# Linear attention and a rational FFN on one core: weight bits joined by shift-and-or, attention from k and r in head pairs, remainders of the first slices on either of two engines, and the order of instructions written out as a list

## The chip, the cores and the metric

The kernel runs on one NeuronCore of a Trainium2 chip. The metric is the time of one execution on the device in microseconds; lower is better. Before the change three runs took 556.85, 558.38 and 558.58 us.

## The reference

Two stages. The first is a linear attention with a decaying state over 768 steps, for 4 batches of 8 heads with 48 dimensions; the second is a feed-forward layer with a rational function between two matrix products.

```python
for t in range(S):                       # B, H, S, D = 4, 8, 768, 48
    kt, vt, rt = (k[:, :, t], v[:, :, t], r[:, :, t])
    cur = np.einsum('bhd,bhe->bhde', u[None] * kt, vt)
    y[:, :, t] = np.einsum('bhd,bhde->bhe', rt, state + cur)
    state = w[None, :, :, None] * state + np.einsum('bhd,bhe->bhde', kt, vt)
...
h = x @ w_in                             # x: 3072 x 384, d_ff = 2048
h2 = h * h
h3 = h2 * h
P = a[0] + a[1] * h + a[2] * h2 + a[3] * h3
Q = 1.0 + np.abs(b[0]) * np.abs(h) + np.abs(b[1]) * h2
g = P / (Q + 1e-06)
return (g @ w_out).astype(np.float32)
```

Both weight matrices arrive as 64-bit floats, which the core sees as pairs of 32-bit words, so the kernel makes 32-bit floats of them out of their bits.

## The kernel before

**Attention.** The 3072 tokens are 24 blocks of 128 (block n is batch n % 4, piece n // 4); two blocks are a pair m, 12 pairs in all. For each block r, k and v are loaded, k and r are multiplied with tables of powers of w (`scale_k`, `scale_r`), the bonus term of u is formed (`bonus_a`, `bonus_b`, `bonus_sum`, `bonus_v`), and k and r are transposed in pairs of heads (`trans`): head q = 0 of a pair of heads comes to partitions 0 to 47, head q = 1 to partitions 64 to 111. `trr_ev` writes the transposed r into two tiles `ys[q]`, whose other partitions later take the masked products of k and r (`a_pe`, `a_ev`: four evictions of 64 partitions a pair). So one matmul over 128 partitions in `y_pe` sums the part of the state and the part of the block's own tokens: `vs` holds state rows and rows of v one above the other. `kv_pe` and `kv_ev` form the states (two chunks of 64 tokens, e = 0 and 1, apart for q), `carry` decays them, `y_ev` adds the bonus.

**Weights.** The two matrices are cut into 28 pieces (12 of 128 x 512 of w_in, 16 of 128 x 384 of w_out). For a piece `cv_load` brings the word pairs, `cv_exp` (ACT) rescales the upper word into PSUM (`cp`), `cv_shift` (DVE) shifts it by 3, `cv_up` and `cv_sign` (ACT) make a second tile `up` with the top bits of the lower word and the sign, and `cv_round` (POOL) adds the two as integers. For every fourth piece DVE puts the sign in (`cv_or`). `cv_hi` and `cv_lo` split the result into a high and a low half in a shorter format.

**FFN.** The tokens are 12 tiles of 256; a tile has 8 slices of 256 of the 2048 columns, 97 slices in all (the last one is cut in two). A slice is: the first product `f1` (tile 0 with whole 32-bit weights, `mm_full`; the others with three products of halves, `mm`), then on ACT Abs, two Squares, Ln and Exp (`ew_z`, `ew_q`, `ew_t`, `ew_ln`, `ew_exp`), on DVE four operations (`ew_u3`, `ew_hi`, `ew_p`, `ew_d`), the remainder `ew_lo` (DVE for slices 0 to 19, POOL from 20 on), and the second product `f2` (`mm2`), which sums up over a tile's slices into two PSUM banks.

**What sets the order.** Every step is a task with a list of what it depends on, of the buffers it takes (`new`) and gives back (`use`), and of the engines that may do it. Before, `order_of` played the program through with given durations and priorities (`PRM`: `OFF`, `CT`, `CS`, `AT`, `X`) and so chose each engine's order, the engine of each task and the PSUM bank; where PE had nothing to do between set times, it put in a matmul on constants (`warm`, line 1135). The engines then run their own lists strictly in order. PSUM has 5 banks `h`, one `pa` and two `o`.

Of the kernel before, what the change touches and what calls it, by code (L numbers as in the profile page):

```python
# [13 lines left out]
F32 = mybir.dt.float32  # L14
# [9 lines left out]
P = 128  # L24
# [5 lines left out]
SMALL = 2.0 ** -40  # L30

PRM = {'AT': (12.19, 36.51, 65.8, 109.86, 123.26, 133.52, 193.98, 232.99, 282.09, 313.75, 378.77, 401.82),
# [6 lines left out]
 'DUE': -79.79,  # L39
 'DX': 8.36,  # L40
 'FULL': (0,),
 'HFREE': 1,
 'MASKED': (),
 'MB': 149.17,
 'NSEG': 4,
 'NT': 1,
 'OFF': {'LV': 270.26,
         'Lk': 774.15,
         'Lr': -796.68,
         'Lv': -312.07,  # L50
         'a': -341.47,
         'ae': 398.71,
         'ba': 33.75,
         'bb': -348.95,
         'beta': -354.71,
         'bs': -201.32,
         'bv': -386.72,
         'c0': -322.33,
         'c2': 127.85,
         'c3': -103.81,  # L60
         'ca': -140.2,
         'ch': 121.32,
         'cl': -34.78,
         'cl_': -128.33,
         'co': -647.77,
         'coef': 293.84,
         'cr': 213.5,
         'cs': -175.01,
         'ctr': -337.17,
         'cu': -134.42,  # L70
         'd': -35.41,
         'ex': -222.41,
         'f1': -18.42,
         'f2': 29.16,
         'flag': -59.53,
         'flagm': 645.83,
         'flagt': 524.35,
         'hi': 12.18,
         'id': 91.47,
         'inv': -624.91,  # L80
         'kv': 150.51,
         'kve': -232.22,
         'ln': 63.38,
         'lo': -1043.9,
         'msk': 27.33,
         'od': 129.99,
         'os': -15.92,
         'p': 68.22,
         'pad': 25.39,
         'pl': 54.79,  # L90
         'pow': -277.52,
         'q': 362.68,
         'rest': 10.15,
         'sk': 150.8,
         'sq': -301.08,
         'sr': -807.06,
         'st0': 436.05,
         't': 292.34,
         'tab': -679.44,
         'tk': 221.19,  # L100
         'tke': 109.8,
         'tr': -205.98,
         'tre': 482.82,
         'turn': -129.33,
         'u3': -36.29,
         'ub': 38.7,
         'ube': -359.69,
         'ubp': -906.35,
         'uw': -294.57,
         'w': -428.73,  # L110
         'w128': -805.12,
         'wl': 257.36,
         'wp': 221.72,
         'x': -170.77,
         'xh': 511.5,
         'xl': 55.87,
         'y': -297.22,
         'ye': 218.13,
         'z': 276.11},
 'PORT': 0.02,  # L120
# [1137 lines left out]
```

## Time and profile before

| | us |
|---|---|
| median of 3 runs | 558.38 |
| lowest, highest | 556.85, 558.58 |
| the profiled execution | 556.55 |
| its span | 554.6 |
| PE busy | 528.4 (95%) |
| DVE busy | 465.9 (84%) |
| ACT busy | 427.8 (77%) |
| POOL busy | 262.9 (47%) |

The profile is of one execution. The span runs from its first instruction to its last; the execution's time is 1.95 us longer. Busy is the time in which an engine had at least one instruction running, and PE's includes the matmuls on constants (31.3 us). The mean granted clock of PE was 0.995 of full speed, and the core moved 35.53 MB. The windows cut the span into stretches with the busy time of each engine; a group's row gives line, engine, operation, output and inputs, count, then total busy us and mean ns of one, then the idle time just before.

### The profile page before, as it was taken

Reading aid. Unit: us, or ns where it says so; the run is one execution under the profiler, and the core shown is the slowest. Engines: PE = TensorE matmul, PEld = TensorE weight load, DVE = VectorE, ACT = ScalarE, POOL = GpSimd, SP = SyncE. Lnnn points to the kernel's source line nnn. Section 1 sums busy time; section 2 is a strip of 40 time slices with the busy share of each in tenths; the row PEclk is TensorE's granted clock in tenths of the full one; section 3 lists DMA queues with packets and bytes.
Section 4 is the critical chain, followed back from the end, with each engine's and each line's share of the span. In section 5 each row is a group of like instructions: output and inputs, shape, how many; then the busy total and the mean of one; then the engine's idle time right before and its main releaser. Section 6 shows DMA issues by size and latency. Waiting matters only on the chain.

```text
span 554.6 us, 14472 instructions
## 1 busy us (share of the span) xinstructions
PE 528.4 (95%) x5817; PEld 509.6 (92%) x5817; DVE 465.9 (84%) x736; ACT 427.8 (77%) x714; POOL 262.9 (47%) x255
## 2 busy tenths in 40 slices
PE   5999869899999999999999999999989999999996
PEld 4988658799999998999999999999989999999996
DVE  5999999899999889789788789688998696786773
ACT  7779888997785796685879585888665788888882
POOL 6766688857431164382445283334354232223221
PEclk9999999999999999999999999999999999999999
DMA  8664667235405007004005200007111000000001
GB/s 225 181 189 124 184 154 201 42 73 112 85 6 116 2 0 153 6 2 102 1 0 114 54 2 31 1 13 158 39 30 31 1 7 23 2 30 1 29 1 36
DMA packets 99503, 35.53 MB, mean 64 GB/s; under 512 B 92770, under 2 KB 95844, under 8 KB 99428
## 3 DMA queue, kind: packets, MB, share of 16 engines
q1 hardware_dynamic: 99428, 34.52, 25.8%
q8 instruction: 48, 0.79, 0.6%
q14 instruction: 27, 0.22, 0.1%
HBM read 29.79 MB, written 4.72 MB: 62 GB/s over the span
## 4 chain that ended last, share of the span: by engine, by line
PE 68%; DVE 20%; ACT 6%; issue 3%; POOL 1%; DMA 1%; SPq 0%; DVEq 0%; ACTq 0%; POOLq 0%
PE h L784 28%; PE o L794 10%; PE o L796 9%; PE o L795 9%; PE warm L1135 3%; DVE ys L703 3%; PE y L743 3%; DVE g L862 2%; DVE h L856 2%; DVE q L866 2%; DVE vs L732 2%; DVE h L872 1%; PE a L689 1%; PE x L760 1%; DVE ys L556 1%
## 5 line engine op out<-in xcount | busy, mean ns | idle before, releaser
L876 POOL TENSOR_TENSOR g<-q,z 128x512 fp32r<-128x512 f32 (+1 forms) x77 | 98.8, 1283 | 192.5 <-DVE q L872 147.0
L784 PE MATMUL h<-xth,whii 128*128 128x256 f32 x528 | 150.2, 284 | 0.0
L784 PE MATMUL h<-xth,wloi 128*128 128x256 f32 x528 | 147.5, 279 | 0.0
L784 PE MATMUL h<-xtl,whii 128*128 128x256 f32 x528 | 147.4, 279 | 0.0
L794 PE MATMUL o<-whio,g 128*128 128x384 f32 x384 | 134.7, 351 | 0.0
L795 PE MATMUL o<-wloo,g 128*128 128x384 f32 x384 | 130.1, 339 | 2.9 <-DVE wloo L553 2.9
L796 PE MATMUL o<-whio,g 128*128 128x384 f32 x384 | 130.2, 339 | 1.0 <-DVE g L876 1.0
L832 ACT ACTIVATE q<-h 128x512 f32<-128x512 f32 (+1 forms) x97 | 57.3, 591 | 77.0 <-PE h L784 76.7
L862 DVE SCALAR_TENSOR_TENSOR g<-h,sig,z 128x512 fp32r<-128x512 f32 (+1 forms) x97 | 72.0, 742 | 47.8 <-ACT z L852 46.2
L784 PEld LDWEIGHTS h<-xth,whii 128*128 128x128 f32 x528 | 99.3, 188 | 0.6
L784 PEld LDWEIGHTS h<-xtl,whii 128*128 128x128 f32 x528 | 99.3, 188 | 0.0
L784 PEld LDWEIGHTS h<-xth,wloi 128*128 128x128 f32 x528 | 99.2, 188 | 0.0
L856 DVE SCALAR_TENSOR_TENSOR h<-t,sig,h 128x512 f32<-128x512 f32 (+1 forms) x97 | 72.0, 743 | 7.4 <-ACT t L843 7.0
L866 DVE SCALAR_TENSOR_TENSOR q<-w,sig,g 128x512 f32<-128x512 f32 (+1 forms) x97 | 72.0, 742 | 5.5 <-DVE g L862 0.5
L795 PEld LDWEIGHTS o<-wloo,g 128*128 128x128 f32 x384 | 72.8, 190 | 3.5 <-DVE wloo L553 3.4
L838 ACT ACTIVATE w<-q,off,root 128x512 f32<-128x512 f32 (+1 forms) x97 | 75.6, 779 | 0.5 <-DVE g L876 0.5
L843 ACT ACTIVATE t<-h,off,root 128x512 f32<-128x512 f32 (+1 forms) x97 | 74.7, 771 | 0.2
L796 PEld LDWEIGHTS o<-whio,g 128*128 128x128 f32 x384 | 72.6, 189 | 1.9 <-DVE g L876 1.9
L794 PEld LDWEIGHTS o<-whio,g 128*128 128x128 f32 x384 | 72.6, 189 | 1.1 <-ACT whio L556 0.2
L848 ACT ACTIVATE z<-w,lnb 128x512 f32<-128x512 f32 (+1 forms) x97 | 66.4, 685 | 7.4 <-POOL m L648 0.4
L852 ACT ACTIVATE z<-z,lnb 128x512 f32<-128x512 f32 (+1 forms) x97 | 69.7, 719 | 2.4
L872 DVE SCALAR_TENSOR_TENSOR q<-h,sig,q 128x512 f32<-128x512 f32 (+1 forms) x77 | 57.0, 740 | 1.8
(147 smaller groups left out, 791.7 us busy)
## 6 DMA issues: line engine op xcount, KB each, us to landing
sti<-in_moe_w_in_dram SPq DMA_DIRECT2D x12, 512.0 KB, 4.8
sto<-in_moe_w_out_dram SPq DMA_DIRECT2D x16, 384.0 KB, 3.2
kh<-in_k_dram SPq DMA_DIRECT2D x24, 192.0 KB, 3.9
rh<-in_r_dram SPq DMA_DIRECT2D x24, 192.0 KB, 4.1
vn<-in_v_dram SPq DMA_DIRECT2D x24, 192.0 KB, 4.1
out_dram<-os SPq DMA_DIRECT2D x24, 192.0 KB, 2.0
vs<-in_v_dram SPq DMA_DIRECT2D x31, 96.0 KB, 3.3
wraw<-in_w_dram SPq DMA_DIRECT2D x1, 1.5 KB
```

The costliest lines, as they stand in the source:

```text
L784: nc.tensor.matmul(o, w_[nm][:, c], x_[:, cc], start=(n == 0), stop=(n == 3 * NCC - 1))
L794: nc.tensor.matmul(o, hi, w_["hi"], start=first, stop=False)
L795: nc.tensor.matmul(o, hi, w_["lo"], start=False, stop=False)
L796: nc.tensor.matmul(o, lo, w_["hi"], start=False, stop=last)
L838: nc.scalar.activation(g["w"], w_, AF.Square, scale=RB, bias=KB)
L843: nc.scalar.activation(g["t"], g["h"], AF.Square, scale=RA, bias=KA)
L848: nc.scalar.activation(g["z"], g["w"], AF.Ln, scale=2.0 ** -LN_SHIFT, bias=lnb[:, 2:3])
L852: nc.scalar.activation(g["z"], g["z"], AF.Exp, scale=-1.0, bias=lnb[:, 1:2])
L856: nc.vector.scalar_tensor_tensor(g["h"], g["t"], KAP, g["h"], op0=ALU.add, op1=ALU.mult)
L862: nc.vector.scalar_tensor_tensor(g["hi"], g["h"], c0, g["z"], op0=ALU.add, op1=ALU.mult)
L866: nc.vector.scalar_tensor_tensor(g["q"], g.get("w", g["q"]), qe, g["hi"].bitcast(F32), op0=ALU.add, op1=ALU.mult)
L876: e.tensor_mul(g["lo"], g["d"], g["z"])
```

## The change

Four things are changed.

1. Weights: `cv_round` on POOL is gone. `cv_join` on DVE shifts and ors in one instruction: `up` now holds bits that an or can set without a carry (scaled by 0.874 with 0.5 added). All 28 pieces take the sign from ACT; `cv_or` isn't used any more.
2. Attention: transposed r goes whole into one tile `rt`, as k does into `kt`; the masked products go to a tile `av` of 128 partitions (two evictions a pair), the states to `st` (one operation for both q), the odd heads' v with its halves of tokens swapped to `vo`, and the even heads' v is read where it was loaded. `y` is summed in two steps: `ys_pe` over the state (48 rows), `y_pe` over the block's own tokens (64 rows), into one PSUM bank for each q, where before there was one for each block. `a_ev` of q = 1 waits for `ys_pe`.
3. The remainder `ew_lo` of slices 0 to 19 may be on POOL or DVE and is written in place of q (`DYN`), as in the later slices.
4. `order_of` and its numbers are gone. `ORDER` is a list of 2194 task numbers, each with a letter for the engine where there is a choice; `placed` follows it. It has no entry for the matmul on constants.

```diff
-        nc.scalar.activation(dst, c["low"].bitcast(U32), AF.Copy, scale=2.0 ** -29)
+        nc.scalar.activation(dst, c["low"].bitcast(U32), AF.Copy, scale=UP * 2.0 ** -29, bias=0.5)
...
-    def cv_shift(c, p):
+    def cv_join(c, p):
         m = c["mag"].bitcast(I32)
         dst = m if on_vector(p) else cv_tile(c, "f", F32).bitcast(I32)
-        nc.vector.tensor_scalar(dst, m, 3, None, op0=ALU.logical_shift_left)
+        nc.vector.scalar_tensor_tensor(dst, m, 3, c["up"], op0=ALU.logical_shift_left, op1=ALU.bitwise_or)
...
-        return p % 4 == 0
+        return p in PRM["VEC"]
...
-    def cv_round(c):
-        bits = c["f"].bitcast(I32)
-        nc.gpsimd.tensor_tensor(bits, bits, c["up"], op=ALU.add)
...
-    def trr_ev(n, e, q):
-        copy(e, ys[q][RROWS[q], n % 2].rearrange("p a t -> p (a t)"), state[n]["tr"][RROWS[q]])
+    def trr_ev(n, e):
+        copy(e, rt[0:TR, n % 2].rearrange("p a t -> p (a t)"), state[n]["tr"][0:TR])
...
-                            ps[q][c, ts(x * NP + p, HALF)], kt[RROWS[q], x, p, c], ys[q][RROWS[q], x, p, c], start=True, stop=True
+                            ps[q][ts(e ^ q, HALF), ts(x * NP + p, HALF)], kt[ROWS[q], x, p, ts(e, HALF)], rt[ROWS[q], x, p, ts(e, HALF)],
+                            start=True, stop=True,
...
+    def a_ev(m, q):
+        mul = nc.vector.tensor_mul(av[:, q], state["a", m, q], mask.unsqueeze(1).to_broadcast([P, 2 * NP, HALF]))
+        if q:
+            for x in range(2):
+                tc.add_manual_dep(mul.ins, state["mm", m, x].ins.name, mybir.DependencyInfo(mybir.DependencyClass.Sync, mybir.DependencyReason.DATA))
...
-            nc.vector.tensor_add(dst, pv, s_[:, chain[e]])
+            nc.vector.tensor_add(s_[:, e + 1], state["kv", m, e], s_[:, e])
...
+    def y_state(m, e, x, p, q):
+        return rt[ROWS[q], x, p, ts(e, HALF)], st[m % 2][ROWS[q], e, x * NP + p]
+
+    def y_own(m, e, x, p, q):
+        rows = ts(e ^ q, HALF)
+        return av[rows, q, x * NP + p], vo[m % 2][rows, x, p] if q else state[2 * m + x]["v"][rows, 2 * p]
+
+    def y_part(m, part, first, last):
+        for x in range(2):
+            for p in range(NP):
                 for e in range(2):
-                    c = ts(e, HALF)
-                    nc.tensor.matmul(pv[c, 2 * p + q], ys[q][:, n % 2, p, c], s_[:, S_[e], p], start=True, stop=True)
+                    if part is y_state and m < 2 and e == 0:
+                        continue
+                    opens_ = x + p == 0 and (first or (m < 2 and e == 0))
+                    for q in (1, 0):
+                        lhs, rhs = part(m, e, x, p, q)
+                        state["mm", m, q] = nc.tensor.matmul(
+                            state["y", m, q][ts(e, HALF), ts(x * NP + p, D)], lhs, rhs, start=opens_, stop=last and (x, p) == (1, NP - 1)
+                        )
...
-        nc.vector.tensor_add(d["m"], d["y"], d["m"])
+        nc.vector.tensor_add(m, state["y", n // 2, q][:, n % 2], m)
...
-            add(("lo", s), lambda e, s=s: ew_lo(s, e), t + 8, {"G": 0.15 + 1.08 * x} if side[s] else {"D": 0.1 + 0.53 * x}, [("d", s)],
+            add(("lo", s), lambda e, s=s: ew_lo(s, e), "GD" if dyn else "G" if side[s] else "D", [("d", s)],
...
-    order, tag_of, _ = order_of(tasks, tags, CAP, PRM)
+    order, tag_of = placed(tasks, tags, CAP)
```

The new function that turns the list into the engines' programs, cut to its core:

```python
def placed(tasks, tags, cap):
    ...
    for tok in ORDER.split():
        if tok[0] == "w":
            order += [("warm", "P")] * int(tok[1:])
            continue
        n = names[int(tok.rstrip(ENGINES))]
        t = tasks[n]
        e = tok[-1] if tok[-1] in ENGINES else t["eng"]
        ...
        order.append((n, e))
```

What this does to the engines' programs, at three places. First PE at the very start, before: transposes of the tables of powers (`tabr`, `tabk`), the spread of u (`us`), and around them matmuls on constants.

```order
L1135 LDWEIGHTS wones
L1135 MATMUL warm<-wones 128x128
L408 MATMUL us_215<-ur,ones 128x384
L457 MATMUL tabk_224<-identw,pk 128x128
L457 MATMUL tabr_199<-identw,pw 128x128
```

The same place after the change, up to the transposes of the first two blocks (`tk`, `tr`):

```order
L346 MATMUL tabr_141<-identw,pw 128x128 x3
L346 MATMUL tabk_176<-identw,pk 128x128
L297 MATMUL us_181<-ur,ones 128x384
L346 MATMUL tabk_176<-identw,pk 128x128 x2
L335 MATMUL wp_191<-wl,identw 48x1 x10
L534 MATMUL tk_206<-identw,kh_104 112x128 x4
L534 MATMUL tr_249<-identw,rh_103 112x128 x4
```

The matmuls on constants, 452 before, are gone, here and between all later pieces of the first slices.

Second POOL ahead of slice 0, before: rounding adds of weight pieces (`wfi`, `wfo`) between the bonus products (`m`) and the state's decay (`vs`).

```order
L547 TENSOR_TENSOR wfo_392<-wfo_392,upo_414 128x384
L653 TENSOR_TENSOR m_535<-m_535,ub 128x384
L547 TENSOR_TENSOR wfi_2_450<-wfi_2_450,upi_2_470 128x512
L553 TENSOR_TENSOR wloo_634<-wfo_392,whio_560 128x384
L662 TENSOR_TENSOR m_535<-vn_369,dt_591 128x384
L547 TENSOR_TENSOR wfi_0_632<-wfi_0_632,upi_0_640 128x512
```

After, the same stretch:

```order
L520 TENSOR_TENSOR m_538<-m_538,ub 128x384
L437 TENSOR_TENSOR wloo_553<-wfo_530,whio_540 128x384
L520 TENSOR_TENSOR m_468<-m_468,ub 128x384
L625 TENSOR_TENSOR st_111<-st_111,w_93 112x384
L437 TENSOR_TENSOR wloi_1_568<-wfi_1_279,whii_1_527 128x512
L750 TENSOR_TENSOR g_547<-q_532,z_543 128x512
```

The adds are gone; low halves of weights (`wloo`, `wloi`) follow each other more closely, and the remainder of slice 0 (L750, output `g`) has come to POOL.

Third DVE in the first slices, before: shifts (L529), an or (L541), masks of the first pair (`ys`, twice each), the sum of `y`.

```order
L703 TENSOR_TENSOR ys_111<-a_0_598,mask 64x8x64 x2
L529 TENSOR_SCALAR wfi_2_682<-cp_652 128x512
L703 TENSOR_TENSOR ys_112<-a_1_599,mask 64x8x64 x2
L553 TENSOR_TENSOR wloo_755<-wfo_638,whio_725 128x384
L748 TENSOR_TENSOR m_358<-y_738,m_358 128x384
L529 TENSOR_SCALAR cp_761<-cp_761 128x384
L748 TENSOR_TENSOR m_535<-y_763,m_535 128x384
L541 SCALAR_TENSOR_TENSOR wfo_798<-sto_656,cp_761 128x384
```

After, around slice 1: shift-and-ors (L417), casts of high halves (`whio`), a mask of 128 partitions (`av`), the remainder no longer among the slice's operations (L730, L736, L740).

```order
L417 SCALAR_TENSOR_TENSOR wfo_670<-cp_578,upo_580 128x384
L440 CAST whio_672<-wfo_670 128x384
L525 TENSOR_REDUCE dt_674<-m_468 128x8
L440 COPY vo_114<-vn_583 64x192
L440 COPY vo_114<-vn_585 64x192
L437 TENSOR_TENSOR wloo_678<-wfo_670,whio_672 128x384
L417 SCALAR_TENSOR_TENSOR wfo_693<-cp_630,upo_690 128x384
L440 CAST whio_695<-wfo_693 128x384
L563 TENSOR_TENSOR av<-a_0_634,mask 128x512
L440 CAST whio_698<-wfo_509 128x384
L730 SCALAR_TENSOR_TENSOR h_561<-t_710,sig,h_561 128x512
L587 TENSOR_TENSOR st_112<-kv_1_588,st_112 112x384
```

Each mask is one instruction where it was two, and casts of high halves, which ACT did before, stand between them: 13 of `whio` on DVE ahead of slice 7, where there was one.

More of the change, by code (lines that the diff above doesn't have):

```diff
@@ L1 @@
-import heapq
 import math
@@ new lines @@
+2169 2178 2171 2183 2172 2161 2135 2148 2149 2162 2163 2173 2174 2175 2179 2181 2182 2184 2185 2176 2186 2187 2188 2191 2189A
+2190 2192A 2193
+"""
+def placed(tasks, tags, cap):
+    names, have, tag_of, uses, order = list(tasks), dict(cap), dict(tags), {}, []
+    for t in tasks.values():
+        for b in t["use"]:
+            uses[b] = uses.get(b, 0) + 1
+    done = set()
+    for tok in ORDER.split():
[3 more added lines that the diff above has]
+        n = names[int(tok.rstrip(ENGINES))]
+        t = tasks[n]
+        e = tok[-1] if tok[-1] in ENGINES else t["eng"]
+        assert e in t["eng"] and len(e) == 1 and done.issuperset(t["deps"]), n
+        for tag, b in t["new"]:
+            if tag == "ps":
+                tag = tag_of[b] = "pa" if have["pa"] > 0 else "h"
+            for x in ("st", "g") if tag == "stage" else (tag,):
+                assert have[x] > 0, n
+                have[x] -= 1
+        for b in t["use"]:
+            uses[b] -= 1
+            if not uses[b]:
+                for x in ("st", "g") if tag_of[b] == "stage" else (tag_of[b],):
+                    have[x] += 1
+        done.add(n)
+        order.append((n, e))
+    assert len(done) == len(names)
+    return order, tag_of
@@ L568, in tile_linear_attention_rational_ffn @@
     TR = HALF + D
-    rh, kh, vs = ([], [], [])
-    vs2 = [cst.tile([P, 5, 2, NP, D], F32, name=f"vs{i}") for i in range(B // 2)]
+    rh, kh = ([], [])
     for i in range(3):
@@ L1028, in build @@
[L1028 to L1031 removed]
+                add(("Lk", n), lambda e, n=n: att_load(n, "k"), "S", [w_("kv", (n - 3) // 2), w_("tk", n - 3), w_("ba", n - 3)])
+                add(("Lr", n), lambda e, n=n: att_load(n, "r"), "S", [w_("tr", n - 2), w_("ba", n - 2)])
@@ new lines, in build @@
+            for h_ in range(len(kvs)):
+                first = m < 2 and h_ == 0
+                add(("kve", m, h_), lambda e, m=m, h_=h_: kv_ev(m, h_, e), "AD" if first else "D",
+                    [("kv", m)] + ([] if first else [("kve", m, 0) if h_ else ("ca", m - 2)]), use=[("kv", (m, h_))])
+            if not last:
+                add(("ca", m), lambda e, m=m: carry(m, e), "GD", [("y", m), ("kve", m, 1), ("w128",)])
+            add(("y", m), lambda e, m=m: y_pe(m), "P", [("ae", m, 0), ("ae", m, 1), ("LV", m, 0), ("LV", m, 1), ("ys", m)],
+                use=vs + [("y", (m, q)) for q in range(2)])
@@ L1069, in build @@
-            side[s] = s in PRM["SIDE"]
-            add(("lo", s), lambda e, s=s: ew_lo(s, e), t + 8, {"G": 0.15 + 1.08 * x} if side[s] else {"D": 0.1 + 0.53 * x}, [("d", s)],
+                add(("f1", s, jj), lambda e, s=s, jj=jj: f1(s, jj), "P",
+                    deps + [(win, p0 + cc) for cc in range(NCC)], new=[] if jj else [("h", h)], use=[("xt", f)] + ([h] if jj else []) + used([p0 + cc for cc in range(NCC)], s, full))
+            add(("z", s), lambda e, s=s: ew_z(s), "A", [("f1", s, nj - 1)], new=[("ta", ("q", s))], use=[h])
@@ L1071, in build @@
                 use=[("q", s), ("z", s), ("g", s)] + ([] if side[s] else [h]))
             for hf in range(2):
-                first = opens(s)
-                new = [("o", ("o", s))] if first and hf == 0 else []
-                so = max(s_ for s_ in range(s + 1) if SL[s_][0] == f and opens(s_))
+                so = next(s_ for s_ in range(s + 1) if SL[s_][0] == f)
+                ob = ("o", so, hf) if f in EXTRA else ("o", so)
+                new = [("h" if f in EXTRA else "o", ob)] if opens(s) and (hf == 0 or f in EXTRA) else []
```

628 lines of the change are left out of this document (212 added, 416 removed), and 9 rows, old and new, of tables (ORDER, PRM).

## The prediction

> **What bounds the kernel now.** I read the windows first, to see which engine is full in which stretch, then the timeline of PE for the price of each piece of work, then the groups for the price of one instruction. All times are of the profiled execution: span 554.6 us, its own time 556.55 us, so 1.95 us lie around the span; the median of the three runs, 558.38 us, is 0.3% above it. In each row below stand, for PE, PEld, DVE, ACT and POOL in this order, the busy time and the count; then the granted clock, the DMA share and GB/s.
>
> ```profile
> 0.00:20.00 20.00, 14.44 (x147) 12.50 (x148) 13.62 (x35) 15.05 (x30) 13.18 (x29) 1.00 0.79 211
> 20.00:112.40 92.40, 80.30 (x1173) 72.38 (x1171) 86.95 (x141) 81.50 (x156) 68.58 (x63) 0.98 0.56 149
> 112.40:200.00 87.60, 86.88 (x1111) 83.52 (x1110) 82.31 (x131) 68.12 (x112) 36.05 (x38) 1.00 0.30 63
> 200.00:542.00 342.00, 339.30 (x3351) 334.05 (x3350) 279.97 (x427) 260.23 (x414) 143.09 (x125) 1.00 0.15 34
> ```
>
> The reader is to see two regimes. From 112 us to 542 us PE is busy 99% of the time, and nothing that shortens DVE, ACT or POOL there can gain more than the idle 3.4 us (0.72 + 2.70). From 20 to 112 us DVE is busy 94% and ACT 88%; PE's 80.30 us hold most of the 31.3 us of warm matmuls, so its real work there is far less. So the first 112 us belong to DVE with ACT close behind, the rest to PE. The boundary is slice 7, the last of tile 0:
>
> ```profile
> 108.06 0.60 ACT L832 ACTIVATE q<-h 128x512 f32<-128x512 f32 x1
> ...
> 542.21 0.39 ACT L832 ACTIVATE q<-h 128x256 f32<-128x256 f32 x1 [1.55 <-PE h L784]
> ...
> 112.40 0.74 DVE L862 SCALAR_TENSOR_TENSOR g<-h,sig,z 128x512 fp32r<-128x512 f32 x1
> ```
>
> Slice 7 leaves its first product at 108.06 us, the last slice at 542.21 us: 434.2 us that PE fills, and 12.4 us of tail. The end is therefore (time at which slice 7 is reached) + (PE work still owed) + tail. Two things can move it: an earlier slice 7, and less PE work.
>
> **The change, part by part: PE.** Prices of PE's pieces, start to start:
>
> ```profile
> 250.35 0.62 PE L667 MATMUL tr<-identw,rh 128*112 128x128 f32 x4
> 250.73 0.42 PE L794 MATMUL o<-whio,g 128*128 128x384 f32 x1
> ...
> 254.05 1.16 PE L689 MATMUL a<-ys,kt 48*64 48x64 f32 x64
> 255.03 0.90 PE L719 MATMUL kv<-vn,kh 64*48 64x48 f32 x64
> 255.86 0.45 PE L794 MATMUL o<-whio,g 128*128 128x384 f32 x1
> ...
> 258.59 0.34 PE L794 MATMUL o<-whio,g 128*128 128x384 f32 x1
> 258.76 0.34 PE L795 MATMUL o<-wloo,g 128*128 128x384 f32 x1
> ...
> 261.30 2.07 PE L743 MATMUL y<-vs,ys 128*64 128x48 f32 x64
> 263.30 0.38 PE L784 MATMUL h<-xth,whii 128*128 128x256 f32 x1
> ```
>
> Four transposes cost 0.38 us, a pair's `a` 0.98 us (64 rows, 15 ns each), `kv` 0.83 us (13 ns), `y` 2.00 us (64 rows, 31 ns). `a` and `kv` use 48 or 64 rows of the array at a time and alternate between its row halves; `y` uses all 128 rows. The change splits `y` in a state part (48 rows, 64 columns wide, alternating row halves, the shape of `a`) and an own part (64 rows): 128 rows a pair in place of 64. At the 15 ns of `a` that is 2 x 0.98 = 1.96 us against 2.00; at 31 ns it is 4.0. I take 15 ns, the row of the nearest shape, so 0 per pair; the ends are 13 ns (1.7 us, -0.3 a pair) and 31 ns (+2.0 a pair). Some nine pairs' worth lies behind slice 7, so -3 to +18 us, value 0. `a` now writes diagonal quarters; its price stays.
>
> At the first product of slice 7 the new order has PE 12 matmuls of the second product further behind (0.17 us each, the step from 258.59 to 258.76; 2.0 us) and 8 transposes ahead (0.8 us): **+1.2 us** still owed. Of the 3.4 us idle behind slice 7 I give back **-1.5 us**, less than half, between 0 and -3.4.
>
> **DVE up to slice 7.** Its rows:
>
> ```profile
> L703 DVE TENSOR_TENSOR ys<-a,mask 64x512 f32<-64x512 f32 x48 | 33.0, 688 | 1.5 <-PE a L689 0.3
> L732 DVE TENSOR_TENSOR vs<-kv,vs 48x384 f32<-48x384 f32 x40 | 22.1, 553 | 0.9
> L876 DVE TENSOR_TENSOR g<-h,z 128x512 fp32r<-128x512 f32 x20 | 13.7, 684 | 0.3
> L748 DVE TENSOR_TENSOR m<-y,m 128x384 f32<-128x384 f32 x24 | 13.0, 549 | 2.0 <-PE y L743 1.9
> L529 DVE TENSOR_SCALAR wfi<-cp 128x512 int32<-128x512 int32 x9 | 6.1, 679 | 0.9 <-ACT cp L524 0.7
> L553 DVE TENSOR_TENSOR wloi<-wfi,whii 128x512 fp32r<-128x512 f32 x4 | 4.9, 1248 | 0.0
> L553 DVE TENSOR_TENSOR wloo<-wfo,whio 128x384 fp32r<-128x384 f32 x5 | 3.3, 662 | 0.7 <-ACT whio L556 0.7
> L640 DVE TENSOR_TENSOR kh<-kh,wkn 128x384 f32<-128x384 f32 x8 | 6.8, 856 | 0.0
> L541 DVE SCALAR_TENSOR_TENSOR wfo<-sto,cp 128x384 int32<-128x384 int32 x4 | 2.2, 543 | 0.0
> L541 DVE SCALAR_TENSOR_TENSOR wfi<-sti,cp 128x512 int32<-128x512 int32 x3 | 2.1, 687 | 0.1
> L556 DVE CAST whii<-wfi 128x512 fp32r<-128x512 f32 x2 | 1.1, 566 | 0.0
> L556 DVE CAST whio<-wfo 128x384 fp32r<-128x384 f32 x1 | 0.4, 359 | 0.0
> ```
>
> Before slice 7's `g`, DVE has 175 instructions now and 162 after the change. The 28 shifts become 28 shift-and-ors of the L541 kind: 0.687 against 0.679 us, so 0. Seven ors go (4.2). Masks go from 12 to 6 twice as tall ones (-4.1 at 0.688), state sums from 8 to 4 (-2.2), low halves of g (L876) from 7 to 0, sent to POOL (-4.8), low halves of weights from 4 and 5 to 2 and 2 (-4.5), scalings from 6 to 2 (-3.3 at L640's price), bonus products and carry from 7 to 2 (-2.9). Casts of weights come over from ACT: 12 more of 0.36 and 4 more of 0.57 (+6.6). The sums of y become 12 of half the width; unshown, between 0.27 (half of L748) and 0.549; I take 0.30, +0.3 (up to +3.3). Two more of xth and one dt: +1.6. Copies of kt, r and v balance out. Sum **-17.5 us**. The means overlap: all DVE groups add up to some 6% more than the busy 465.9 us, so it is -16.5 us of engine time.
>
> **ACT up to slice 7.**
>
> ```profile
> L556 ACT CAST whio<-wfo 128x384 fp32r<-128x384 f32 x15 | 7.6, 504 | 0.9 <-POOL wfo L547 0.7
> L556 ACT CAST whii<-wfi 128x512 fp32r<-128x512 f32 x10 | 6.1, 606 | 1.0 <-POOL wfi L547 1.0
> L515 ACT ACTIVATE upo<-sto 128x384 f16<-128x384 f32 x12 | 7.6, 632 | 0.0
> L594 ACT COPY vs<-zero 64x576 f32<-64x576 f32 x6 | 4.0, 666 | 0.1
> ```
>
> Its 177 instructions ahead of slice 7's Abs become 149: 12 and 5 casts less (-9.0), no zeroing of the state (-4.0), copies of k, r, v and x less (-5.3), 6 sign writes more (+4.2), and +0.2 for two others: **-13.9 us**, -13 of engine time. ACT has 12% of idle time in this stretch as cover; with DVE relieved, ACT is what is late next, and 13 us is about all it yields.
>
> **POOL and the queues.**
>
> ```profile
> L547 POOL TENSOR_TENSOR wfo<-wfo,upo 128x384 int32<-128x384 int32 x16 | 17.2, 1080 | 5.0 <-ACT upo L515 2.9 <-DVE h L872 1.7 <-ACT upo L511 0.3
> L547 POOL TENSOR_TENSOR wfi<-wfi,upi 128x512 int32<-128x512 int32 x12 | 15.8, 1316 | 7.7 <-ACT upi L515 5.3 <-DVE ys L556 1.6 <-ACT upi L511 0.7
> L876 POOL TENSOR_TENSOR g<-q,z 128x512 fp32r<-128x512 f32 (+1 forms) x77 | 98.8, 1283 | 192.5 <-DVE q L872 147.0
> ```
>
> The rounding adds, 33.0 us of POOL, go, and with them one step of 1.1 to 1.3 us in each piece's chain. In their place POOL takes eighteen more low halves at 1.283 (23.1 us in all, 9 of them ahead of slice 7), so it stays below its present 74% in that stretch, and I cost this at 0; without that cover each low half is 0.6 us later than on DVE, in front of a second product that PE runs several slices behind. SP issues the same blocks in another order and two fewer; the 18 MB of the first 112 us need 190 GB/s if they must be there by 97 us, and the first row above shows 211. Cost 0.
>
> **The sum.** If DVE alone set the pace at its present 94%, slice 7 would come 17 us earlier; by ACT, 13 us; if a new wait eats it, 0. I take 11.5, a little under ACT's figure, because both engines are now equally loaded and wait for each other. 556.55 - 11.5 + 1.2 - 1.5 + 0 = 544.8, so **545 us**, against its own 556.55.
>
> **The rivals.** *PE slows down without warm matmuls (slower).*
>
> ```profile
> 66.00:69.00 3.00, 1.52 (x5) 1.52 (x6) 2.97 (x5) 2.09 (x4) 1.60 (x2) 0.70 0.98 249
> 69.00:72.00 3.00, 3.00 (x40) 2.75 (x38) 2.87 (x6) 2.52 (x5) 1.49 (x2) 0.73 0.35 83
> 78.00:81.00 3.00, 1.01 (x7) 0.74 (x6) 2.89 (x6) 2.98 (x6) 2.54 (x4) 1.00 0.58 158
> ...
> 553.00:554.60 1.60, 0.00 (x0) 0.00 (x0) 0.00 (x0) 0.00 (x0) 0.00 (x0) 0.50 0.02 5
> ...
> L1135 PE MATMUL warm<-wones 128*128 128x128 bf16 x452 | 31.3, 233 | 2.1 <-POOL wones L352 2.1
> ```
>
> After a pause of PE the clock was 0.70 and 0.73, though with 1.01 us of work in 3 it also stayed at 1.00; 0.50, the lowest that the trace has, stands behind the last matmul. The change drops all 452 warm matmuls. PE's real work up to slice 7 is 50.5 us at full clock, by the prices above and the order; with slice 7 at 97 us and the first transposes at 8 us there are 89 us for it, so PE becomes the bound below a mean clock of 0.57. At 0.50 it needs 101 us, slice 7 comes at 109 at the earliest and with its dependent stalls some 5 us later than now: 556.55 + 1.2 + 5 = 563. Against it: from the first slice on, 37 of the 50.5 us fall into some 60 us, a far larger share than in the row that kept 1.00. Chance 0.13. The Trainium skill, page "TensorE: Matmul & The Clock Gate", section "What's actually happening", says that the clock is halved by default and after an idle window of about 3.4 us; by that rule the first 35 us, where PE has 13 us of work, would run at half rate. The two rows at 0.70 agree with it in kind.
>
> *The own part of y does not pack.* In it each bank of y is written from both row halves in turn; the rows of `a` and `kv` show each bank fed from one half only. If that runs at 31 ns, it costs 1.0 us a pair, +9 us behind slice 7: 554. Chance 0.13. The Trainium skill, page "TensorEngine Tiling (Array Packing)", section "Gotcha 1: PSUM Pressure", states that different row tiles cannot access the same PSUM bank at the same time, which would make it so; no run here shows it yet.
>
> *The early gain does not arrive* (new waits between ACT, DVE and POOL): 556.55 + 1.2 - 1.5 = 556. Chance 0.12. *All of it arrives*: DVE's 17, the whole 3.4 and cheap y: 556.55 - 17 + 1.2 - 3.4 - 3 = 534. Chance 0.06. My forecast, 540 to 550, has 0.56.
>
> **How the numbers follow.** Faster by over 0.3% (about what a measurement tells from no change): the forecast, the full gain, and half each of the packing and the no-gain case, 0.74. Within 0.3%: 0.10. Slower: the clock and the worse ends of y, 0.16. The range takes in the full gain but for its last microsecond and reaches beyond the packing and no-gain cases: 535 to 560.
>
> **What would show it.** Right: slice 7's Abs at 94 to 100 us; from there to the last slice's Abs 432 to 436 us; the state and own parts of y near 1 us a pair each; no L547 kind on POOL. Wrong: a granted clock under 0.8 between 40 and 100 us with PE busy throughout; an own part near 2 us; a slice 7 later than 105 us with DVE and ACT both below 85% busy, which would say that the waits between them, not their work, set the pace.

## The result and the profile after

The changed kernel took **543.64 us** (median of 4 runs, 543.12 to 545.3) against 557.62 us before (4 runs): a ratio of 0.9756, 95% interval 0.9723 to 0.9789, so 14 us faster. The prediction said 545.0 us. The profiled execution is the slowest of the four (545.3 us, 1.7 above the median), and the one before was faster than its median (556.55 us, 1.1 below), so the difference of the two profiles, 11.25 us, is 2.7 us smaller than that of the medians.

The head of the page, then the windows, cut at the same places as before (the first product of slice 7 is followed by its `g` at 102.68 us now); columns as in the prediction:

```profile
span 543.6 us, 14777 instructions
PE 511.5 (94%) x6069; PEld 492.5 (91%) x6069; DVE 424.3 (78%) x692; ACT 405.9 (75%) x670; POOL 254.9 (47%) x242
```

```profile
0.00:20.00 20.00, 8.76 (x48) 5.87 (x48) 12.30 (x28) 13.54 (x30) 9.14 (x23) 1.00 0.80 214
20.00:102.68 82.68, 69.43 (x967) 61.95 (x968) 73.53 (x135) 70.87 (x127) 57.28 (x57) 0.86 0.62 165
102.68:200.00 97.32, 96.10 (x1141) 93.69 (x1140) 81.19 (x125) 73.32 (x116) 51.81 (x47) 1.00 0.22 47
200.00:532.00 332.00, 330.94 (x3882) 325.06 (x3881) 254.12 (x400) 245.22 (x393) 134.16 (x117) 1.00 0.14 32
```

Up to slice 7's `g` DVE has 12.30 + 73.53 = 85.8 us of work (100.6 before) and ACT 84.4 (96.6 before); DVE is busy 89% of the second stretch (94% before), ACT 86% (88%). Behind it PE is full as it was. The timeline of ACT and DVE gives the same marks as before, start and duration:

```profile
97.91 0.58 ACT L706 ACTIVATE q<-h 128x512 f32<-128x512 f32 x1
...
531.90 0.37 ACT L706 ACTIVATE q<-h 128x256 f32<-128x256 f32 x1
```

```profile
102.68 0.75 DVE L736 SCALAR_TENSOR_TENSOR g<-h,sig,z 128x512 fp32r<-128x512 f32 x1
```

Slice 7's Abs comes at 97.91 us in place of 108.06, 10.15 us earlier. From there to the last slice's Abs it is 433.99 us (434.15 before), and the tail is 11.7 us (12.4). So all but a microsecond of the 11 us between the two spans lies ahead of slice 7.

The costliest groups of DVE up to 98 us, and then two views of `y`: the timeline of PE (a state part begins at 148.31, an own part lies between the second and third row), and the chain of work, which gives the time from the start of such a block to the next one:

```profile
L417 DVE SCALAR_TENSOR_TENSOR wfo<-cp,upo 128x384 int32<-128x384 int32 x15 | 8.2, 549 | 0.1
L417 DVE SCALAR_TENSOR_TENSOR wfi<-cp,upi 128x512 int32<-128x512 int32 x12 | 8.0, 677 | 0.1
L440 DVE CAST whio<-wfo 128x384 fp32r<-128x384 f32 x12 | 7.8, 654 | 0.1
...
L621 DVE TENSOR_TENSOR m<-y,m 128x192 f32<-128x192 f32 x12 | 3.7, 348 | 2.1 <-PE y L605 2.1
```

```profile
148.31 1.15 PE L605 MATMUL y<-st,rt 48*64 48x48 f32 x64
...
155.78 0.25 PE L605 MATMUL y<-vo,av 64*64 64x48 f32 x1
...
156.71 0.22 PE L605 MATMUL y<-vn,av 64*64 64x48 f32 x1
```

```profile
148.38 1.08 PE y L605 x64
...
155.85 1.08 PE y L605 x64
```

Each part of a pair costs 1.08 us, 17 ns a matmul, so a pair 2.16 us against 2.00 before. The joins wait 0.2 us in all. The casts cost 0.654 us where the prediction took 0.36. Three stretches of 3 us show the clock (the column after the bracket of POOL):

```profile
27.00:30.00 3.00, 2.91 (x68) 2.58 (x67) 1.48 (x5) 2.52 (x5) 1.05 (x2) 0.50 1.04 335
45.00:48.00 3.00, 3.00 (x57) 2.88 (x51) 2.90 (x8) 3.00 (x7) 0.82 (x1) 0.50 0.98 267
...
60.00:63.00 3.00, 2.08 (x113) 1.85 (x105) 2.77 (x6) 2.12 (x5) 3.00 (x3) 1.00 0.40 137
```

The granted clock is 0.50 also in 3 us in which PE is busy throughout, and is back at 1.00 from 60 us on. The 1.00 of the first 20 us can't be taken at its word. Of the two rows that follow, four transposes each, the second lies where the clock was 0.59 (30 to 33 us), and both take 1.06 us, against 0.62 us in the prediction's row at 250.35:

```profile
15.60 1.06 PE L534 MATMUL tr<-identw,rh 128*112 128x128 f32 x4
...
30.86 1.06 PE L534 MATMUL tk<-identw,kh 128*112 128x128 f32 x4
```

So PE ran slowly at the start too, and the column is read only from 20 us on.

### The profile page after: what moved, and what is told of

Read it like the earlier page. It is cut to its first block, busy times and chain, and to the rows that moved or that the text cites. A ratio compares the mean times of both kernels' runs of the same rounds, so it can differ in the third digit from the quotient of the medians.

```text
span 543.6 us, 14777 instructions
## 1 busy us (share of the span) xinstructions
PE 511.5 (94%) x6069; PEld 492.5 (91%) x6069; DVE 424.3 (78%) x692; ACT 405.9 (75%) x670; POOL 254.9 (47%) x242
## 4 chain that ended last, share of the span: by engine, by line
PE 75%; DVE 3%; ACT 1%; issue 0%; POOL 0%; DVEq 0%; POOLq 0%; ACTq 0%
PE h L658 32%; PE o L668 11%; PE o L670 11%; PE o L669 11%; PE y L605 3%; PE a L555 2%; PE kv L576 2%; PE tk L534 1%; PE x L633 1%; PE tr L534 1%; DVE q L740 1%; DVE g L736 1%; ACT z L726 0%; DVE h L730 0%; DVE q L746 0%
## 5 line engine op out<-in xcount | busy, mean ns | idle before, releaser
L750 POOL TENSOR_TENSOR g<-q,z 128x512 fp32r<-128x512 f32 (+1 forms) x95 | 123.2, 1297 | 225.9 <-DVE q L746 152.1
L736 DVE SCALAR_TENSOR_TENSOR g<-h,sig,z 128x512 fp32r<-128x512 f32 (+1 forms) x97 | 72.1, 744 | 46.1 <-ACT z L726 40.7
L730 DVE SCALAR_TENSOR_TENSOR h<-t,sig,h 128x512 f32<-128x512 f32 (+1 forms) x97 | 71.8, 742 | 17.3 <-ACT t L717 11.6
L717 ACT ACTIVATE t<-h,off,root 128x512 f32<-128x512 f32 (+1 forms) x97 | 73.7, 769 | 12.6 <-PE h L658 12.5
L740 DVE SCALAR_TENSOR_TENSOR q<-w,sig,g 128x512 f32<-128x512 f32 (+1 forms) x97 | 72.1, 743 | 6.1
L746 DVE SCALAR_TENSOR_TENSOR q<-h,sig,q 128x512 f32<-128x512 f32 (+1 forms) x97 | 72.1, 743 | 2.7
```

What stands on the lines that cost most here:

```text
L717: nc.scalar.activation(g["t"], g["h"], AF.Square, scale=RA, bias=KA)
L730: nc.vector.scalar_tensor_tensor(g["h"], g["t"], KAP, g["h"], op0=ALU.add, op1=ALU.mult)
L736: nc.vector.scalar_tensor_tensor(g["hi"], g["h"], c0, g["z"], op0=ALU.add, op1=ALU.mult)
L740: nc.vector.scalar_tensor_tensor(g["q"], g.get("w", g["q"]), qe, g["hi"].bitcast(F32), op0=ALU.add, op1=ALU.mult)
L746: nc.vector.scalar_tensor_tensor(g["d"], g["h"], c0, g["q"], op0=ALU.add, op1=ALU.subtract)
L750: e.tensor_mul(g["lo"], g["d"], g["z"])
```

## The experiments

All medians are of 4 to 10 runs; the kernel before took 557.9 to 558.0 us beside them (557.62 beside the changed kernel). The table reads each run as the prediction does: when slice 7 is reached, and how long PE takes from there to the last slice's Abs (both from the timeline of ACT of the profiled execution). Up to slice 30 e12 runs the instructions of the changed kernel, and its slice 7 is 1.6 us later, so differences of that size in the column say nothing.

| run | us | slice 7's Abs | to the last Abs |
|---|---|---|---|
| before | 557.62 | 108.06 | 434.15 |
| after | 543.64 | 97.91 | 433.99 |
| e1, old rounding | 570.63 | 118.89 | 437.77 |
| e2, DVE +17 us | 558.84 | 109.56 | 434.92 |
| e3, ACT +16 us | 554.20 | 106.66 | 434.94 |
| e4, adds aside | 568.24 | 118.72 | 437.47 |
| e5, y in runs | 601.05 | 114.49 | 473.73 |
| e6, after with warm matmuls | 544.01 | 98.10 | 434.30 |
| e7, all the work, old planner | 564.54 | 100.22 | 449.79 |
| e8, join alone, old planner | 577.20 | 117.66 | 445.18 |
| e9, POOL +20 us | 558.85 | 103.95 | 442.57 |
| e10, join alone, old order | 566.02 | 116.81 | 435.53 |
| e11, before without warm | 561.70 | 111.42 | 435.79 |
| e12, DVE +21 us late | 556.00 | 99.49 | 444.98 |

### Which engine sets the time of slice 7: e2 and e3

```diff
+        nc.vector.tensor_scalar(dst, m, 3, None, op0=ALU.logical_shift_left)
         nc.vector.scalar_tensor_tensor(dst, m, 3, c["up"], op0=ALU.logical_shift_left, op1=ALU.bitwise_or)
```

> The changed kernel with one more shift on DVE ahead of each of the 28 joins (12 x 0.68 + 16 x 0.55 = 17.0 us, nothing else), written where the join writes afterwards. If DVE sets the pace up to slice 7: the end 13 to 17 us later, 557 to 561 us. If DVE and ACT set it together (the prediction's view): 9 to 14 us later, 553 to 558 us. If waits between engines or the arrival of the weights set it, DVE's idle time takes most of it: 0 to 5 us, 544 to 549 us.

```diff
         nc.scalar.activation(c["mag"], c["top"].bitcast(F32), AF.Copy, scale=2.0 ** -112)
+        nc.scalar.activation(c["mag"], c["top"].bitcast(F32), AF.Copy, scale=2.0 ** -112)
```

> The changed kernel with each piece's first ACT step done twice in a row (12 x 0.63 + 16 x 0.53 = 16.1 us of ACT, nothing else; the result is the same). If ACT sets the pace up to slice 7: 13 to 16 us later, 556 to 560 us. If DVE and ACT set it together: 9 to 13 us later, 552 to 557 us. If DVE alone does: 0 to 5 us, 543 to 549 us.

With 17.0 us more on DVE the time is 558.84 us (ratio to before 1.0028, 1.0008 to 1.0049; after 0.9756), +15.2 by medians and +12.75 by profiles; slice 7 moves by 11.65. With 16.1 us more on ACT it is 554.20 us (0.9928, 0.9906 to 0.995), +10.6 and +9.9; slice 7 moves by 8.75. The windows from 20 us to slice 7's Abs, first of the changed kernel, then of e2 and of e3 (the third and fourth busy times are DVE and ACT):

```profile
20.00:97.91 77.91, 65.96 (x941) 58.66 (x942) 69.03 (x128) 66.19 (x119) 54.04 (x54) 0.85 0.66 174
```

```profile
20.00:109.56 89.56, 71.89 (x944) 63.26 (x944) 82.69 (x153) 67.07 (x118) 53.80 (x54) 0.87 0.57 152
```

```profile
20.00:106.66 86.66, 68.72 (x952) 59.88 (x952) 69.59 (x129) 80.33 (x147) 54.62 (x54) 0.86 0.60 158
```

Neither engine hides behind the other: both set the pace, DVE more. By its median e2 lies where I had put DVE alone; e3 lies where I had put the two together. Counted from 0 to slice 7's Abs, e2 has 15.0 us more of DVE (96.35 against 81.32), which is what the kernel before had (96.39), and e3 has 14.8 us more of ACT (94.56 against 79.72; 92.21 before). So either load, put back alone, takes back most or all of the 10.15 us: both had to go for the gain. The two rates (11.65 of 15.0 us and 8.75 of 14.8) can't be added up: for the 15.1 us of DVE and 12.5 us of ACT that the change takes off they would make 19 us. Both runs leave the time behind slice 7 within 1 us of what it was.

### Does DVE's idle time behind slice 7 cover added work: e12

```diff
         nc.vector.scalar_tensor_tensor(g["hi"], g["h"], c0, g["z"], op0=ALU.add, op1=ALU.mult)
+        if s in range(30, 58):
+            nc.vector.scalar_tensor_tensor(g["hi"], g["h"], c0, g["z"], op0=ALU.add, op1=ALU.mult)
```

> The changed kernel with 28 more instructions on DVE (0.74 us each, 20.8 us) where PE is the bound: the high half of g is made twice in slices 30 to 57; nothing else. If only the time up to slice 7 belongs to DVE, and behind it DVE's idle time covers this: 542.5 to 546 us. If DVE's steps lie in the path there too: 550 to 562 us.

It took 556.00 us (0.9964, 0.9946 to 0.9981), +12.4: my reading of that stretch as PE's alone, with DVE's idle time as cover, was wrong for work that is added. The three largest of PE's waits in e12 between 120 and 530 us (total, times, longest), and the whole stretch of the changed kernel and of e12:

```profile
PE h L658 <- DVE q L742: 2.1, 5, 0.8
PE a L555 <- DVE q L742: 1.2, 2, 0.9
PE tk L534 <- DVE q L742: 0.9, 2, 0.6
```

```profile
97.91:532.00 434.09, 430.50 (x5047) 422.04 (x5047) 339.82 (x531) 323.22 (x518) 189.21 (x166) 1.00 0.16 35
```

```profile
99.49:545.00 445.51, 435.18 (x5050) 423.52 (x5050) 359.55 (x560) 323.68 (x519) 190.19 (x166) 1.00 0.15 34
```

DVE is busy 78% of that stretch in the changed kernel, and in e12 in no 20 us of the loaded part (200 to 340 us) over 92%. Yet 19.7 us more of it lengthen the stretch by 11 us. PE's waits for DVE between 120 and 530 us go from 1.1 to 8.0 us, and PE is busy 4.7 us longer for the same matmuls. I read this so, without a further test: the order lets PE arrive just when DVE is done, so a fixed list has little slack in either engine although one shows 22% idle.

### The joining of the weight bits: e1, e4, e9, e10, e8

e1 puts the add on POOL back, in the new order:

```diff
-        nc.scalar.activation(dst, c["low"].bitcast(U32), AF.Copy, scale=UP * 2.0 ** -29, bias=0.5)
+        nc.scalar.activation(dst, c["low"].bitcast(U32), AF.Copy, scale=2.0 ** -29)
...
-        nc.vector.scalar_tensor_tensor(dst, m, 3, c["up"], op0=ALU.logical_shift_left, op1=ALU.bitwise_or)
+        nc.vector.tensor_scalar(dst, m, 3, None, op0=ALU.logical_shift_left)
+        nc.gpsimd.tensor_tensor(dst, dst, c["up"], op=ALU.add)
```

> The changed kernel with the old way of joining the weight bits: DVE only shifts (same price as the shift-and-or, 0.55 and 0.68 us), and POOL adds the second tile as integers, 28 adds of 1.08 and 1.32 us (33 us of POOL) behind the DVE step of each piece. Everything else keeps its place. By the prediction (POOL has room, term 0): slice 7's Abs within 1 us of 97.9 us and a time of 542 to 546 us. Rival: the step of 1.1 to 1.3 us in each piece's chain, and its place in POOL's queue, is what made the early part slow before: slice 7's Abs at 103 to 109 us, time 548 to 555 us.

e4 keeps the join and does the adds beside it:

```diff
         nc.vector.scalar_tensor_tensor(dst, m, 3, c["up"], op0=ALU.logical_shift_left, op1=ALU.bitwise_or)
+        nc.gpsimd.tensor_tensor(c["up"], dst, c["up"], op=ALU.add)
```

> The changed kernel with the same 28 integer adds on POOL as in the run with the old rounding (33 us, behind each piece's DVE step), but written back into the second tile, which nothing reads: the casts and low halves no longer wait for them; the second tile's buffer is still held until the add is done, as there. The shift-and-or stays. If the casts' wait for POOL (the step in the chain) made that run 27 us slower: 543 to 549 us. If POOL's time and the held buffer did: 558 to 572 us. In between, the share says which part is which.

e9 loads POOL without holding the second tile:

```diff
         e.tensor_sub(cv_tile(c, "lo", F32R), c["f"], c["hi"].bitcast(F32))
+        if e is nc.gpsimd:
+            e.tensor_sub(c["lo"], c["f"], c["hi"].bitcast(F32))
```

> The changed kernel with each low half of the weights that POOL makes made twice in a row (24 of 28; ahead of slice 7, 11 x 1.03 + 6 x 1.48 = 20 us of POOL). No second tile is held by it and the casts don't wait for it. The runs with 33 us of integer adds on POOL came 25 and 27 us later. If POOL's time alone made them so: 20 of 33 us give 14 to 17 us, 558 to 561 us. If the held buffer of the second tile did, for which ACT waits there (10.2 us of its idle time in the run with the adds aside): 0 to 5 us, 543 to 549 us.

e1 took 570.63 us (1.0230, 1.0207 to 1.0252), e4 568.24 (1.0186, 1.0167 to 1.0205), e9 558.85 (1.0030, 1.0011 to 1.0049). Of the 27 us of e1 only 2.4 are the casts' wait for the add; the rest stays when nothing waits for its result. So neither my 0 nor the rival's price for the step in the chain holds in the new order, and e1 lies outside both of its ranges: nearly all of it comes from POOL's time and from the second tile that the adds hold. e9, without a held tile, lies in the range of POOL's time alone. What ACT waited for in e4 between 20 and 119 us, then the windows up to slice 7 of e4 and of e9, and one behind it of e9 (the last busy time is POOL):

```profile
ACT upo L400 <- POOL upo L418: 6.5, 4, 3.3
...
ACT upo L400 <- POOL upi L418: 2.2, 2, 1.4
```

```profile
20.00:118.72 98.72, 74.63 (x940) 63.87 (x941) 75.07 (x128) 67.02 (x121) 81.20 (x78) 0.84 0.53 138
```

```profile
20.00:103.95 83.95, 66.96 (x938) 58.17 (x939) 75.49 (x128) 67.03 (x121) 67.96 (x66) 0.86 0.62 163
...
100.00:120.00 20.00, 14.48 (x91) 13.34 (x90) 14.64 (x19) 13.00 (x22) 19.37 (x18) 0.91 0.09 20
```

In e9 slice 7 is 6.0 us later, and POOL is then full; the stretch behind it is 8.6 us longer, and PE's largest waits there are for low halves that POOL makes (for the changed kernel the view lists none):

```profile
PE o L671 <- POOL wloo L439: 4.3, 2, 3.6
```

In e4 slice 7 is 20.8 us later; at least 8.7 us of ACT's waits there are for second tiles that POOL still holds. And in both, DVE is busy some 6 us longer than the 69.03 us of the changed kernel with the same 128 instructions. Most of that is in casts and copies between SBUF tiles (in e9 the casts to `whio` take 9.8 us in place of 7.8, those to `whii` 5.0 in place of 3.6, the copies to `vo` 2.0 in place of 0.4): POOL's work slows DVE's (the last section shows how). How much of e4 is queueing on POOL, how much the held tile, was not separated further.

e10 comes from the other side. It takes the kernel before with each engine's order frozen (PE's list is the same to the instruction) and puts in the join alone, on DVE where the sign is written on ACT; e8 lets the planner order the same work anew:

```diff
-            add(("c2", p), lambda e, c=c, p=p: cv_shift(c, p), t + 0.3, {"D": 0.1 + 0.53 * x}, [("c0", p)], new=[] if sv else fw, use=cp)
...
+            add(("cr", p), lambda e, c=c, p=p: cv_shift(c, p), 0, {"D": 0}, [("cs", p)], new=[(tag, ("wf", p))], use=[("cp", p), ("up", p)])
...
+                new += {"c0": [(n, "A")], "cu": [(n, "A")] + ([] if ("cs", p) in names else [(("cs", p), "A"), (("cr", p), "D")]), "cs": [(n, "A"), (("cr", p), "D")]}.get(k, [])
```

> The kernel before with the shift-and-or alone (28 integer adds on POOL and 7 ors on DVE less, 7 sign writes on ACT more), but with every engine's order kept as the planner made it for the kernel before: PE's list is the same to the instruction, warm matmuls included, and the join stands on DVE where its sign is written on ACT. In the run where the planner ordered it anew the time was 577 us. If that came from the new order alone, and POOL's adds cost nothing in the kernel before (term 0): 554 to 559 us. If the adds on POOL held the early slices back: 543 to 552 us. If the 7 sign writes or the later DVE step hurt: 560 to 577 us.

> The kernel before with the shift-and-or alone: no integer adds on POOL (33 us less), no separate ors on DVE (4.2 us less), 7 sign writes more on ACT (about 4.5 us more), same planner. By the prediction's terms (POOL 0; DVE 4 less against ACT 4 more): 554 to 559 us. If the step on POOL in each piece's chain held the early slices back in the kernel before too: 543 to 551 us.

e10 took 566.02 us (1.0143, 1.0123 to 1.0164), e8 577.20 (1.0351, 1.0332 to 1.0370): 33 us of POOL and 7 ors less, and slower by 8 and 19 us. e10 lies in its third range; e8 lies outside both of its own, and why it is so much slower than e10 (9.7 us of it behind slice 7) stays open. What DVE waited for in e10 between 20 and 112 us:

```profile
DVE wfi L560 <- ACT upi L546: 7.8, 6, 2.1
DVE wfo L560 <- ACT upo L546: 6.5, 6, 1.4
```

Before, the add on POOL waited for the second tile (2.9 and 5.3 us behind ACT's L515 in POOL's rows of the prediction), and POOL had room to wait. The join waits for the same tile on DVE, which has none: 14.3 us, and slice 7 is 8.75 us later. In the changed kernel the joins wait 0.2 us: its list puts each one where the sign is already there. In both orders in which it was tried by itself the join is a loss; in the written-out order its wait is gone.

### All of the work in the old planner's order: e7

```diff
-    order, tag_of = placed(tasks, tags, CAP)
+    order, tag_of = planned(tasks, tags, CAP, SL, JG, NT, NG, NS, FULL)
```

`planned` gives the tasks the priorities and durations of the kernel before and calls its `order_of`.

> All the work of the changed kernel (join, attention, remainders), but ordered by the planner and the numbers of the kernel before, with matmuls on constants and with the durations given for the new tasks; its numbers aren't searched again. If the work saved on DVE, ACT and POOL brings the gain in any reasonable order: 541 to 548 us. If the written-out order is what turns saved work into time: 552 to 562 us.

It took 564.54 us (1.0114, 1.0091 to 1.0138), above both ranges and 21 us more than with the written-out list. Slice 7 comes at 100.22 us, 7.8 us earlier than before, but with more work left for later: behind it stand 449.79 us. One group of PE from 100.2 us on, in e7 and in the changed kernel:

```profile
L803 PE MATMUL y<-st,rt 48*64 48x48 f32 x640 | 11.5, 219 | 0.0
```

```profile
L605 PE MATMUL y<-st,rt 48*64 48x48 f32 x576 | 10.3, 219 | 0.0
```

Ten pairs of attention are left in e7, nine in the changed kernel as before the change. Of the 15.8 us that the stretch is longer than there, 14.5 are time in which PE is busy (444.86 against 430.40 us, with 298 more matmuls), not waits. A pair is some 5 us (2.16 for `y`, 0.98 and 0.83 for `a` and `kv` by the prediction's rows, and its transposes); 31 more matmuls of the first product are 3.6 (0.117 us each by the chain); a mean clock of 0.77 from 415 to 430 us, where the changed kernel has 1.00, is worth up to 3.4. The rest is open. The planner's numbers weren't searched again for the new work, so this is not its best; it shows that the saved work doesn't bring the gain in every order. The opposite case, the written-out way of ordering with the old attention or the old remainders, was not run, so what each of these two parts brings by itself isn't shown.

### The clock: e6 and e11

```diff
+WARM = {("tk", 0): 14, ("kv", 0): 36, ("y", 0): 8, ("x", 0): 4, ("f1", 0, 0): 6, ("kv", 1): 20, ("a", 1): 16}
...
+        order += [("warm", "P")] * WARM.get(n, 0)
```

> The changed kernel with 104 matmuls on constants put in front of PE tasks before which PE stands idle between 13 and 44 us (14, 36, 8, 4, 6, 20 and 16 of them; 5.8 us at full clock), to lift the granted clock of 0.74 and 0.66 in the windows from 20 to 60 us. If the half clock there costs time (the rival of the slowed PE): granted clock above 0.9 from 20 to 46 us and the end 2 to 6 us earlier, 537 to 542 us. If DVE and ACT set the pace and the clock cost nothing: 542 to 545 us.

```diff
-            if n_ == "warm":
-                nc.tensor.matmul(warm[:, 0:P], wones, wones, start=True, stop=True)
-            else:
+            if n_ != "warm":
```

> The kernel before, every engine's order kept, without its 452 matmuls on constants. If they hold the clock up where it counts: granted clock of 0.6 to 0.8 between 20 and 60 us, slice 7's Abs 2 to 6 us later, time 560 to 564 us. If DVE and ACT set the pace there and the clock costs nothing: 556 to 559 us, with the low clock all the same.

e6 took 544.01 us (0.9744, 0.9720 to 0.9768), the same as the changed kernel; e11 561.70 (1.0065, 1.0041 to 1.0088), 3.8 us more than before, as its first range said. The windows of the changed kernel, of e6 and of e11:

```profile
20.00:46.00 26.00, 19.73 (x394) 17.28 (x394) 21.96 (x49) 20.89 (x38) 14.63 (x18) 0.74 0.79 208
46.00:60.00 14.00, 12.26 (x171) 10.93 (x166) 10.87 (x21) 11.77 (x23) 11.51 (x13) 0.63 0.86 219
```

```profile
20.00:46.00 26.00, 21.99 (x457) 19.66 (x458) 21.62 (x45) 20.08 (x36) 14.35 (x17) 0.87 0.79 199
46.00:60.00 14.00, 10.86 (x177) 9.29 (x171) 11.40 (x23) 12.43 (x24) 10.86 (x12) 0.76 0.88 236
```

```profile
40.00:60.00 20.00, 12.76 (x111) 10.48 (x111) 18.04 (x28) 16.85 (x32) 11.58 (x11) 0.79 0.52 136
```

The same four transposes in the kernel before and in e11, whose column reads 1.00 from 20 to 40 us against what the second row shows:

```profile
25.42 0.65 PE L667 MATMUL tk<-identw,kh 128*112 128x128 f32 x4
```

```profile
25.68 1.10 PE L667 MATMUL tk<-identw,kh 128*112 128x128 f32 x4
```

In the kernel before the warm matmuls were worth 3.4 us at slice 7 (111.42 against 108.06). DVE's waits for PE between 20 us and slice 7 go from 1.0 us to 3.5 in e11, the sum of `y` alone from 0.5 to 1.9: PE's steps lie between DVE's there, and at a lower clock they hold DVE up. In the changed kernel raising the clock from 0.74 to 0.87 and from 0.63 to 0.76 brought nothing. It came neither to the 0.9 that the expectation asked for nor to 1.00, so what a full clock would bring stays open.

### The order of y's matmuls: e5

```diff
-        for x in range(2):
-            for p in range(NP):
-                for e in range(2):
...
-                    for q in (1, 0):
+        for q in (1, 0):
+            for e in range(2):
...
+                for x in range(2):
+                    for p in range(NP):
```

> The changed kernel with the matmuls of y in another order: eight in a row on the same rows and columns of the array (head half and token half outside, block and pair of heads inside), where the change alternates from matmul to matmul. The same matmuls, the same sums. If alternation is what lets them run at 15 ns a row of the list, each part of a pair goes from about 1 us to about 2 (the old price of 31 ns): +2 us a pair, +16 to +20 us for the pairs behind slice 7, 560 to 566 us. If the price doesn't hang on the order: 542 to 546 us.

It took 601.05 us (1.0757, 1.0722 to 1.0793). Its chain of work, a state part and an own part:

```profile
309.34 3.31 PE y L605 x64
317.82 3.28 PE y L605 x64
```

In runs a matmul takes 52 ns, in alternation 17. Nine pairs at 6.59 in place of 2.16 us make 39.9 us; behind slice 7 the run is 39.7 us longer. Both expected values missed: alternation matters, and by twice what I thought. The Trainium skill, page "TensorE: Matmul & The Clock Gate", section "The mechanism", says that a weight load overlaps a running matmul only where their groups of rows differ. The 52 ns and the 17 ns of the state part, where the rows change with every matmul, agree. The 17 ns of the own part don't follow from it: every second of its matmuls has the same rows as the one before it, and other columns.

## Why the prediction was right, point by point

- **The sum**: 544.8 us, and the profiled execution took 545.3. Its 11.25 us are 10.15 ahead of slice 7, 0.16 behind it, 0.7 in the tail and 0.25 around the span; the last two were not forecast and fill most of what slice 7 fell short of, which is luck.
- **Slice 7 earlier by 11.5 us**: 10.15 in the profile. The relief of DVE up to slice 7's `g` was 14.7 us (16.5 predicted) and ACT's up to its Abs 12.5 (13). On DVE the mis-sized term is the casts that came over from ACT: 12 at 0.654 in place of 0.36 us, 3.5 us; the other terms together relieved 1.7 us more than forecast. e2 and e3 show that the two loads set the time of slice 7 together, which is the step's reason for a figure a little under ACT's. The size, 11.5, was a choice and not worked out from a rate.
- **PE work owed, +1.2, and idle given back, -1.5**: neither shows in the stretch, and with opposite signs they cancelled, which is luck. PE's busy time from slice 7 to the last Abs is 430.50 us (430.73 before), and its idle time 3.6 (3.4): nothing was given back.
- **y, 0**: 2.16 in place of 2.00 us a pair, 1.4 us for nine pairs. The value was nearly right, the upper end was not: I bounded the price by 31 ns, the old `y`, but that row alternated too, between halves of columns. Without alternation it is 52 ns, and the term could have been +41 us where I allowed +18.
- **POOL, 0**: right as a net only. I wrote that the adds go and low halves come, and that POOL keeps its cover. e4 and e9 show that POOL's time is not free in this order (25 and 15 us for 33 and 29 us of it), so the adds had to go for the low halves to move; e10 shows that removing them alone, with the join on DVE in their place, gains nothing and costs 8 us.
- **The clock rival**: its mechanism came (0.50 in places, and a slow start by the transposes) and did not decide; the mean from 20 us to slice 7's Abs was 0.85, above the 0.57 at which I said it would. That bound was worked out too low: the rows of the kernel before give PE 90.4 - 31.3 = 59.1 us of work up to slice 7, not the 50.5 that I added up from prices, and 59.1 of 89 us is 0.66. That the clock can cost something shows in e11.
- **The packing rival**: refuted by the trace; the own part costs the 1.08 us of the state part.
- **No early gain**: it did not come here, but it is what happens in an order that isn't fitted to the work. All of the work in the old planner's order takes 564.5 us (e7), and the join alone 566 and 577 (e10, e8). The saving of 11.5 us was read from engine loads. That it arrives needs a list without the waits that e10 suffers; the new list is one (0.2 us), and the prediction took this for granted.

## What to carry to other kernels

Under a fixed order of instructions, an engine's saved time is worth what the order makes of it: look not only at what an operation costs but at which engine now does the waiting, and whether that engine has room for it. Idle time on an engine behind a full one is no proof of slack, and adding to it can be tested cheaply by doing an instruction twice whose second execution changes nothing. The price of small matmuls is to be taken from a row that alternates between parts of the array in the same way: here 17 ns in alternation and 52 without.

## What was not expected of the hardware

**A cast between SBUF tiles on DVE waits for POOL's running instruction.** The timeline of DVE, then of POOL, in the changed kernel:

```profile
34.60 0.35 DVE L440 CAST whio<-wfo 128x384 fp32r<-128x384 f32 x1
...
78.59 1.43 DVE L440 CAST whio<-wfo 128x384 fp32r<-128x384 f32 x1
```

```profile
78.09 1.72 POOL L437 TENSOR_TENSOR wloi<-wfi,whii 128x512 fp32r<-128x512 f32 x1
```

The same cast takes 0.35 us alone; the one at 78.59 takes 1.43 and ends 0.21 us after POOL's instruction does. The other casts of weights that take 0.70 us or more between 20 and 102 us do so too, 0.22 to 0.29 us after an instruction of POOL. The Trainium skill, page "SBUF — State Buffer", section "SBUF: two separate sides", says that a pair of ports is shared by the two engines and locked for a whole instruction, and the rows agree. So a cast moved from ACT to DVE costs up to four times its price where POOL is busy.

**Two row halves of the array write one PSUM bank with no loss.** In the own part each bank takes both row halves in alternation, and it costs the 1.08 us of the state part, where each bank has one. The Trainium skill, page "TensorEngine Tiling (Array Packing)", section "Gotcha 1: PSUM Pressure", says that different row tiles cannot access the same PSUM bank at the same time. Here four matmuls, two for each bank and from both row halves, start within 0.02 us (155.78 to 155.80 us), and no loss shows; so the measurement decides, for outputs that lie on different partitions. When each of them writes, the profile does not show.
